# One tiled stretch a phase over eight PSUM banks, with an earlier softmax and a reordered start, in an attention-plus-MLP kernel

## The chip, the cores and the metric

One core of one Trainium2 chip. The metric is device microseconds of one execution, median of several; lower is better. The four runs of the kernel before agree within 0.3%. All spans, waits and instruction times come from the hardware profile.

## The reference, cut to what matters

```python
# x: (8, 8, 512, 64), state: (8, 8, 32, 64); per batch b and head h
a      = softmax(x @ state.T / 8)        # 512 x 32
xread  = a @ state                       # 512 x 64
a2     = softmax(state @ x.T / 8)        # 32 x 512
sread  = a2 @ x                          # 32 x 64
tokens = concat(xread, sread)            # 8 batches x 544 rows, 512 columns
out    = silu(tokens @ w_in) @ w_out     # w_in 512 x 2048, w_out 2048 x 512
```

The kernel never builds xread. As xread @ w_in = a @ (state @ w_in), it builds per batch a small product W1 = blockdiag(state) @ w_in (four quarters of 512 columns), transposes a, and uses W1 and aT in the first layer. "g" is silu of the first layer. The 32 sread rows of each batch are gathered and go through the MLP at the end, as a ninth small batch.

## The kernel before

Matmuls write to PSUM. The kernel has eight PSUM tiles of 128 x 512 fp32, called banks here: o0, o1, w0, w1, h0, h1, a0, a1. A bank can be written again only when an engine has copied its content out; that is what "frees a bank" means below. The instruction order on each engine is the order of these calls; nothing is rescheduled. ([...] marks cuts.)

```python
def w1_m(b, j, bks):        # one W1 quarter: 8 matmuls on 64x32 tiles of the array, two banks
    for kt in range(KT):
        for half in range(2):
            nc.tensor.matmul(bank[bks[half]][ds(32 * kt, 32), :], [...],
                             tile_position=(64 * half, 32 * kt))
def w1_e(b, j, bks, engs):  # copy both banks to W1 in SBUF, by ACT or DVE
    [...]
# sread_m: 32 matmuls on 128x32 tiles; sread_n: divide, on DVE; sread_t: transpose
# sc/scs: scores; ex/exs: exp on ACT; norm_s: row sums on DVE; norm_m: a = e / sum, DVE or POOL
# a_T: transpose of a on PE; a_Td: the same by DMA; x_Td: transpose of x by DMA

def g1(b, ft):              # a first-layer tile: 2 matmuls 128x512, then SiLU on ACT frees the h bank
    bk = bank[f"h{hctr[0] % 2}"]
    [...]
    nc.scalar.activation(g[b % 2][:, ft, :], bk[:], func=SILU, bias=0.0)

def o_e(b, tt, bk, eng="dve", [...]):   # copy a finished output bank to SBUF, then DMA it out
    [...]
    cp(eng, t[:, c0:c1], bank[bk][:, c0:c1])

def W1p(b, i):
    for j in range(2):
        w1_m(b, 2 * i + j, WP[j])           # WP = (("w0","w1"), ("h0","h1"))
    [...]

def phase(k, fill):          # 64 output matmuls of batch k; `fill` is put between them
    for tt in range(4):
        bk = ("o0", "o1")[tt % 2]
        for ft in range(16):
            g2(k, tt, ft, bk)
            for f in fill.get(16 * tt + ft, ()):
                f()
        o_e(k, tt, bk)

def att_tail(fill, b, s, a0, sg, dg):      # work for batch b, during phase b - 1
    add(fill, s, L(exs, b), L(W1p, b, 0))
    add(fill, s, L(norm_s, b, 0, 2), L(norm_m, b, "pool", 0, 2))
    add(fill, s, L(norm_s, b, 2, 2), L(norm_m, b, "dve", 2, 2))
    add(fill, s, L(nc.scalar.preload_act_table, SILU))
    add(fill, s + 14, L(W1p, b, 1), L(sread_m, b, "a1"), L(sread_n, b, "a1"))
    [...]
```

The prologue prepares batches 0 and 1 together (casts, transposes, scores, softmax). In the first phase (outputs of batch 0) W1 is built quarter by quarter for both batches.

The softmax here doesn't subtract the row's maximum and nothing guards it: scores larger than these inputs give would overflow.

## Time and profile before

| | before |
|---|---|
| time, median of 4 runs | 221.52 us |
| span in the profile | 219.67 us |
| first output matmul | 17.7 us |
| first phase / second phase | 28.0 / 26.95 us |
| a steady phase (third to sixth) | 23.14 us |

The page of the kernel before, busy time of the engines and the chain of waits that ended last:

```profile
PE 209.2 (95%) x1652; PEld 104.2 (47%) x1678; DVE 84.0 (38%) x171; ACT 131.5 (60%) x221; POOL 40.7 (19%) x78
...
PE 90%; DMA 2%; SPq 2%; issue 1%; ACT 1%; DVE 1%; POOL 0%
```

TensorE (PE) binds: it is hardly ever idle, and the chain runs through it. The busy share hides one thing: the profile models a 128x512 matmul as 379 ns, but starts are 0.216 us apart, so time on PE is counted by starts.

The timeline of PE around the two tiled stretches of one phase of the kernel before (start, duration, engine, line, operation, out<-in, shape, count, then idle time before it and what ended that):

```profile
95.75 0.59 PE L296 MATMUL ps_o<-w_out_sb,g 128*128 128x512 bf16 x2
96.28 0.41 PE L251 MATMUL ps_w<-w_in_sb,sbd 64*32 64x512 bf16 x8
96.50 0.56 PE L251 MATMUL ps_h<-w_in_sb,sbd 64*32 64x512 bf16 x8
97.23 2.97 PE L296 MATMUL ps_o<-w_out_sb,g 128*128 128x512 bf16 x13 [0.16 <-issue]
100.13 0.41 PE L251 MATMUL ps_w<-w_in_sb,sbd 64*32 64x512 bf16 x8
100.35 0.40 PE L251 MATMUL ps_h<-w_in_sb,sbd 64*32 64x512 bf16 x8
100.68 0.43 PE L218 MATMUL ps_a<-x_n,en 128*32 128x65 bf16 x32
```

The last full-array matmul before the first stretch starts at 95.97, the first tile at 96.28 instead of 96.19: entering costs 0.09 us, leaving about 0.10. Eight W1 tiles run together and cost 0.22. Counting by starts, the two stretches push their neighbours apart by 0.83 and 1.02 us. In the first of them 0.16 is neither: the second half of its h group starts at 96.66, when ACT's SiLU, which held that bank, has ended (96.61). (Each "x13" and the like misses one matmul record just after a stretch; its weight load is in the trace and was used.)

The timeline of PE at the start of the kernel before, three of its rows:

```profile
14.05 0.41 PE L251 MATMUL ps_o<-w_in_sb,sbd 64*32 64x512 bf16 x8
...
15.89 0.81 PE L272 MATMUL ps_h<-aT,W 128*128 128x512 bf16 x3
...
17.87 0.59 PE L296 MATMUL ps_o<-w_out_sb,g 128*128 128x512 bf16 x2
```

The busy times by stretch of the kernel before; the stretches begin at the first weight load of an output matmul of each phase (columns: stretch, its length, then busy time and instructions of PE, PE weight loads, DVE, ACT, POOL, granted clock, DMA share, GB/s):

```profile
0.00:17.66 17.66, 13.63 (x207) 11.06 (x208) 11.19 (x30) 11.26 (x22) 10.49 (x20) 1.00 0.89 201
17.66:45.66 28.00, 27.41 (x204) 11.55 (x207) 10.34 (x24) 16.27 (x30) 7.81 (x13) 1.00 0.96 168
45.66:72.61 26.95, 26.69 (x212) 12.55 (x215) 10.93 (x22) 19.87 (x31) 4.27 (x9) 1.00 0.59 167
72.61:95.75 23.14, 22.88 (x176) 10.47 (x178) 9.80 (x19) 15.27 (x24) 4.27 (x9) 1.00 0.45 126
```

### The profile page before, as it was taken

The page shows a single profiled execution, that of the slowest core. Times are in us where ns is not written, and L with a number is a line of the kernel's source. Part 1 is how long each engine was busy: PE and PEld are TensorE (multiplying, and loading weights), DVE is VectorE, ACT ScalarE, POOL GpSimd, SP SyncE. Part 2 cuts the span into 40 slices and gives each one's busy share as a digit, 9 for nine tenths or more (in the row PEclk, how much of TensorE's full clock was granted, in tenths as well). Part 3 has the DMA queues.
Part 4 walks back from the last instruction along what each step waited for, and adds up shares of the span by engine and source line. Part 5 has one row for each costly group of instructions (what it writes and reads, how often), then busy time and mean ns, then how long its engine had stood idle before and what let it go on. Part 6 is the DMA issues. An engine that isn't in the chain of part 4 may idle for free.

```text
span 219.7 us, 4129 instructions
## 1 busy us (share of the span) xinstructions
PE 209.2 (95%) x1652; PEld 104.2 (47%) x1678; DVE 84.0 (38%) x171; ACT 131.5 (60%) x221; POOL 40.7 (19%) x78
## 2 busy tenths in 40 slices
PE   7779999999999999999999999999999999999993
PEld 7555334453544444444444444444443444566552
DVE  4767321445730672139312841087107600111110
ACT  3873766669677846776477837692669277433210
POOL 1778222001600070007000610043001000000000
PEclk9999999999999999999999999999999999999999
DMA  6899999289551138512770269015411311111112
GB/s 204 229 179 169 206 232 188 42 225 286 191 120 51 48 97 189 196 48 51 187 243 3 69 169 276 16 51 145 95 48 51 97 48 51 49 48 48 51 48 96
DMA packets 36868, 26.56 MB, mean 121 GB/s; under 512 B 20848, under 2 KB 32368, under 8 KB 36848
## 3 DMA queue, kind: packets, MB, share of 16 engines
q1 hardware_dynamic: 30160, 20.39, 32.8%
q0 software_dynamic: 6128, 5.44, 14.8%
q10 hardware_dynamic: 560, 0.46, 0.6%
q8 instruction: 13, 0.21, 0.4%
q14 instruction: 7, 0.06, 0.1%
HBM read 17.30 MB, written 8.91 MB: 119 GB/s over the span
## 4 chain that ended last, share of the span: by engine, by line
PE 90%; DMA 2%; SPq 2%; issue 1%; ACT 1%; DVE 1%; POOL 0%
PE ps_o L296 49%; PE ps_h L272 25%; PE ps_w L296 4%; PE ps_h L283 3%; DMA x_f<-in_x_dram 2%; PE ps_w L251 2%; PE ps_h L251 2%; PE ps_a L218 1%; SPq L91 1%; PE ps_a L160 1%; PE ps_a L251 1%; ACT x_n L83 1%; PE ps_a L202 1%; DVE W L79 1%; POOL an L186 0%
## 5 line engine op out<-in xcount | busy, mean ns | idle before, releaser
L296 PE MATMUL ps_o<-w_out_sb,g 128*128 128x512 bf16 x462 | 124.8, 379 | 2.3 <-issue 1.7
L280 ACT ACTIVATE g<-ps_h 128x512 bf16<-128x512 f32 x128 | 75.7, 598 | 51.9 <-PE ps_h L272 49.6
L272 PE MATMUL ps_h<-aT,W 128*128 128x512 bf16 x248 | 73.6, 379 | 0.5 <-DVE W L79 0.3
L296 PEld LDWEIGHTS <-g 128*128 128x128 bf16 x512 | 47.9, 98 | 51.8 <-issue 1.6
L79 DVE COPY o_sb<-ps_o 128x512 f32<-128x512 f32 x30 | 20.6, 689 | 91.7 <-PE ps_o L296 76.7
L272 PEld LDWEIGHTS <-W 128*128 128x128 bf16 x256 | 24.3, 98 | 29.7 <-issue 1.6
L186 POOL TENSOR_TENSOR an<-en,rs 128x512 bf16<-128x512 bf16 x9 | 9.5, 1060 | 110.8 <-ACT W L83 56.6
L81 POOL CAST x_u<-x_f 128x256 bf16<-128x256 f32 x44 | 17.8, 447 | 4.5 <-DMA x_f<-in_x_dram 4.5
L79 DVE CAST W<-ps_w 128x512 bf16<-128x512 f32 x24 | 15.3, 679 | 3.5 <-PE ps_w L251 3.5
L83 ACT ACTIVATE W<-ps_h 128x512 bf16<-128x512 f32 x24 | 13.1, 603 | 0.1
L291 ACT ACTIVATE g_s<-ps_h 128x256 bf16<-128x256 f32 x16 | 6.1, 383 | 11.2 <-PE ps_h L283 11.2
L181 DVE TENSOR_REDUCE rs<-en 128x16 f32<-128x512 bf16 x16 | 10.5, 659 | 3.2 <-ACT en L171 3.1
L79 DVE CAST W<-ps_a 128x512 bf16<-128x512 f32 x7 | 4.8, 691 | 14.2 <-PE ps_a L251 14.2
L283 PE MATMUL ps_h<-xsT,w_in_sb 128*128 128x256 bf16 x64 | 9.6, 273 | 0.0
L296 PE MATMUL ps_w<-w_out_sb,g 128*128 128x512 bf16 x32 | 9.5, 379 | 0.1
L283 PEld LDWEIGHTS <-w_in_sb 128*128 128x128 bf16 x64 | 6.3, 98 | 4.1
L160 PEld LDWEIGHTS <-xT 128*128 128x128 bf16 x128 | 5.9, 98 | 4.3 <-DVE xT L79 0.4
L251 PEld LDWEIGHTS <-sbd 64*32 64x32 bf16 x256 | 3.1, 88 | 9.9 <-issue 9.4
L508 ACT ACT_TABLE_LOAD x6 | 7.7, 1283 | 0.1
L171 ACT ACT_TABLE_LOAD x6 | 7.7, 1283 | 0.1
L321 PEld LDWEIGHTS <-zeros 128*128 128x128 bf16 x86 | 6.6, 116 | 2.3 <-DVE zeros L335 1.2
L171 ACT ACTIVATE en<-ps_a 128x512 bf16<-128x512 f32 (+1 forms) x14 | 7.3, 564 | 0.4 <-PE ps_a L160 0.2
(66 smaller groups left out, 126.7 us busy)
## 6 DMA issues: line engine op xcount, KB each, us to landing
out_dram<-o_sb SPq DMA_DIRECT2D x32, 256.0 KB, 2.3
x_f<-in_x_dram SPq DMA_DIRECT2D x5, 1024.0 KB, 6.7
x_f<-in_x_dram SPq DMA_DIRECT2D x8, 256.0 KB, 4.5
w_in_sb<-in_moe_w_in_dram POOLq DMA_DIRECT2D x4, 512.0 KB, 9.6
w_out_sb<-in_moe_w_out_dram POOLq DMA_DIRECT2D x4, 512.0 KB, 11.9
x_f<-in_x_dram POOLq DMA_DIRECT2D x1, 1024.0 KB, 18.1
out_dram<-o_sb ACTq DMA_DIRECT2D x1, 256.0 KB, 2.5
st_nat<-in_state_dram POOLq DMA_DIRECT2D x6, 32.0 KB, 13.1
```

The lines of the kernel that those rows point to most:

```text
L79: nc.vector.tensor_copy(dst, src)
L81: nc.gpsimd.tensor_copy(dst, src)
L83: nc.scalar.activation(dst, src, func=COPY, bias=0.0)
L160: nc.tensor.matmul(v[:, kt % 2, :, c, :], xT[b % 2][:, kt, c, :], sbd[:, b, kt, :, :], start=True, stop=True, skip_group_check=True,)
L171: nc.scalar.activation(en[b % 2][:, :, :, ds(kt, n), :].rearrange("p h c k s -> p k (h c) s"), v[:, ds(kt % 2, n)], func=EXP, bias=0.0, sc ...
L181: nc.vector.tensor_reduce(v, en[b % 2][:, :, :, ds(kt, n), :], axis=AX, op=ADD)
L186: e.tensor_tensor(an[b % 2][:, :, :, ds(kt, n), :].rearrange("p h c k s -> p (h c) k s"), en[b % 2][:, :, :, ds(kt, n), :].rearrange("p h ...
L251: nc.tensor.matmul(bank[bks[half]][ds(32 * kt, 32), :], sbd[ds(64 * half, 64), b, kt, half, :], w_in_sb[ds(64 * half, 64), kt, ds(512 * j, ...
L272: nc.tensor.matmul(bk[:], W1[b % 2][:, half, ds(128 * ft, 128)], aT[b % 2][:, half, :, :], start=(half == 0), stop=(half == 1), skip_group ...
L280: nc.scalar.activation(g[b % 2][:, ft, :], bk[:], func=SILU, bias=0.0)
L283: nc.tensor.matmul(bk[:, 0:256], w_in_sb[:, kt, ds(128 * ft, 128)], xsT[:, kt, :, :, :], start=(kt == 0), stop=(kt == KT - 1), skip_group_ ...
L296: nc.tensor.matmul(bank[bk][:, c0:c1], src[:, ft, ds(128 * tt, 128)], w_out_sb[:, ft, c0:c1], start=(ft == 0), stop=(ft == 15), skip_group ...
```

## The change

Its intent: enter and leave the tiled shape once a phase instead of twice, by giving all four W1 quarters and sread a bank of their own (eight banks); have the softmax done well before the stretch; and start the first phase sooner, by taking batch 1 out of the prologue and loading the first weights ahead of batch 1's x. The diff cut to its core:

```diff
@@ later phases
-        def phase(k, fill):
-                bk = ("o0", "o1")[tt % 2]
+        TB = ("w0", "o0", "w1", "o1")        # four output banks in turn
+        def phase(k):
+                o_e(k, tt, TB[tt])
+                for f in fill.get((4 * k + tt,), ()):
+                    f()
+        def tiled(b, tt):                     # right behind the output copy tt
+            cur, nxt, third, srb = (TB[(tt + i) % 4] for i in range(4))
+            bks = ((srb, nxt), HB, AB, (third, cur))
+            for j in range(4):
+                w1_m(b, j, bks[j])
+            w1_e(b, 0, bks[0], ("act", "dve"))
+            sread_m(b, srb)
+            for j in range(1, 4):
+                w1_e(b, j, bks[j], ("act", "dve"))
+            sread_n(b, srb)
+        def soft(b):                          # all of it queued at once
+            exs(b)
+            nc.scalar.preload_act_table(SILU)
+            for q, e in enumerate(("pool", "dve")):
+                norm_s(b, 2 * q, 2)
+                norm_m(b, e, 2 * q, 2)
+            a_Td(b)
+            if b + 1 < B:
+                cast_xu(b + 1)
+        # step = 64 * phase + 16 * output + matmul. Per batch: x transpose, state transpose
+        # and x copy, scores, softmax, stretch (behind output number), sread transpose,
+        # first first-layer tile, steps between these tiles
+        plan = {
+            2: (None, None, 68, 74, 5, 108, 104, 1.5),
+            3: (98, 108, 119, 128, 9, 172, 166, 1.4),
+            4: (152, 172, 183, 188, 12, 225, 219, 1.5),
+        }
+        for b in range(5, B):
+            p = 64 * (b - 2)
+            plan[b] = (p + 20, p + 30, p + 46, p + 51, 4 * (b - 1), p + 97, p + 91, 1.5)
@@ start
-        nc.scalar.dma_start(st_f[0][:], ...)     # state of batch 1 came later, on SP
+        for b in range(2):
+            nc.scalar.dma_start(st_f[b][:], ...)
         ... x of batch 0 ...
-        ... x of batch 1 on SP ...
+        load_wi(0); load_wo(0); load_wi(1); load_wo(1)
+        load_x(1, nc.gpsimd, 0, 2)                # second half later, behind these
+        cp("act", st_nat[:, 1, :], st_f[1][:])    # ahead of everything else on ACT
@@ first phase: batch 1's casts, transposes, scores, softmax go here; W1 in pairs
+        w1_m(1, 1, AB)
+        w1_m(1, 2, HB)
+        w1_e(1, 2, HB, DA)
+        w1_e(1, 1, AB, DA)
   [...]
+        w1_m(0, 3, AB)
+        w1_m(1, 3, HB)
```

Also, batch 2's a is now transposed by DMA (a_Td) instead of on PE.

More of the change, by code (lines that the diff above doesn't have):

```diff
@@ L151, in x_Td, with x_nu @@
         )
+    def x_nu(b):
         nc.vector.tensor_copy(
@@ L326 @@
     with tc.manual_schedule():
-        nc.scalar.dma_start(st_f[0][:], state[0].rearrange("h ns d -> ns h d"))
+        for b in range(2):
+            nc.scalar.dma_start(st_f[b][:], state[b].rearrange("h ns d -> ns h d"))
         for kt in range(KT):
             load_x(0, nc.sync, kt, 1)
-        for kt in range(KT):
-            if kt == 2:
-                nc.sync.dma_start(st_f[1][:], state[1].rearrange("h ns d -> ns h d"))
-            load_x(1, nc.sync, kt, 1)
+        make_identity(nc, ident[:])
+        cp("pool", st_nat[:, 0, :], st_f[0][:])
+        load_wi(0)
+        load_wo(0)
+        load_wi(1)
+        load_wo(1)
+        load_x(1, nc.gpsimd, 0, 2)
         nc.vector.memset(zeros[:], 0.0)
@@ L338 @@
             nc.vector.memset(x_n[i][:, :, :, 1:131:129], 1.0)
-        make_identity(nc, ident[:])
         nc.scalar.preload_act_table(EXP)
@@ L346 @@
         HB = ("h0", "h1")
-        OB = XB
+        OB = ("w0", "w1", "o0", "o1")
         DA = ("dve", "act")
@@ L359, in exs, with xTs @@
         def exs(b):
-            for q in range(2):
-                ex(b, 2 * q, 2, AB[q])
+            ex(b, 0, 2, "a0")
+            ex(b, 2, 2, "a1")
+        def xTs(b, q, eng):
+            for kt in (2 * q, 2 * q + 1):
+                x_T(b, kt, AB[q])
+            x_Te(b, 2 * q, 2, AB[q], eng)
         def scs(b, q):
@@ L368 @@
         cast_x(0, "dve", (0,))
-        cp("pool", st_nat[:, 0, :], st_f[0][:])
+        cp("act", st_nat[:, 1, :], st_f[1][:])
         x_T(0, 0, XB[0])
@@ L373 @@
         st_T(0, "a1", "act", "dve")
-        cast_x(0, "dve", (2,), (0,))
-        cast_x(0, "pool", (2,), (1,))
-        cast_x(0, "dve", (3,), (0,))
-        cast_x(0, "pool", (3,), (1,))
-        cast_x(1, "pool", (0,), (1,))
-        load_wi(0)
-        load_wo(0)
+        cast_x(0, "dve", (2,))
         warm(8, "w1")
@@ L383 @@
         x_Te(0, 1, 1, XB[1], "act")
+        cast_x(0, "dve", (3,))
         sc(0, 0, SB[0])
         ex(0, 0, 1, SB[0])
-        warm(8, "w1")
+        warm(10, "w1")
         x_T(0, 2, XB[2])
         x_Te(0, 2, 1, XB[2], "act")
+        x_T(0, 3, XB[3])
+        x_Te(0, 3, 1, XB[3], "dve")
         sc(0, 1, SB[1])
         ex(0, 1, 1, SB[1])
-        warm(3, "w1")
-        x_T(0, 3, XB[3])
-        cast_x(1, "dve", (0,), (0,))
-        x_Te(0, 3, 1, XB[3], "dve")
-        warm(3, "o0")
+        warm(9, "o0")
         for kt in (2, 3):
@@ L398 @@
             ex(0, kt, 1, SB[kt])
-        cast_x(1, "dve", (1,))
-        cast_x(1, "act", (2,))
         norm_s(0, 0, 2)
         norm_m(0, "pool", 0, 2)
-        x_T(1, 0, "o0")
-        x_T(1, 1, "o0")
-        x_Te(1, 0, 2, "o0", "dve")
-        cp("act", st_nat[:, 1, :], st_f[1][:])
-        cast_x(1, "act", (3,))
-        warm(8, "a0")
-        st_T(1, "a1", "dve", "dve")
-        norm_s(0, 2, 2)
-        norm_m(0, "pool", 2, 2)
-        x_T(1, 2, "o1")
-        x_T(1, 3, "o1")
-        x_Te(1, 2, 2, "o1", "act")
-        warm(4, "a0")
-        sc(1, 0, "w0")
-        sc(1, 1, "w0")
-        ex(1, 0, 2, "w0")
-        warm(8, "a0")
-        sc(1, 2, "w1")
-        sc(1, 3, "w1")
-        ex(1, 2, 2, "w1")
-        nc.scalar.preload_act_table(SILU)
-        warm(8, "a0")
+        norm_s(0, 2, 2)
+        norm_m(0, "dve", 2, 2)
+        nc.scalar.preload_act_table(SILU)
+        st_T(1, "h0", "act", "act")
+        warm(6, "o0", 512)
+        w1_m(0, 0, ("w0", "w1"))
+        w1_m(1, 0, ("o0", "o1"))
+        w1_e(0, 0, ("w0", "w1"), ("act", "act"))
         a_T(0, (("a0", "dve"), ("a1", "dve")))
-        W1x(0, 0, ("o0", "o1"), DA)
-        load_wi(1)
-        load_wo(1)
+        w1_e(1, 0, ("o0", "o1"), DD)
+        warm(2, "h1", 512)
+        load_x(1, nc.gpsimd, 2, 2)
         load_wi(2)
         load_wo(2)
-        norm_s(1, 0, 2)
-        norm_m(1, "pool", 0, 2)
-        norm_s(1, 2, 2)
-        norm_m(1, "dve", 2, 2)
-        warm(6, "o0")
         g1(0, 0)
         g1(0, 1)
-        sread_m(0, "a0")
-        sread_n(0, "a0")
+        sread_m(0, "a1")
+        sread_n(0, "a1")
         g1(0, 2)
         g1(0, 3)
+        G2(0, 0)
+        sread_t(0, "a1", "dve")
+        G2(0, 1)
+        W1x(0, 1, AB, DA)
+        G2(0, 2)
+        G2(0, 3)
+        for i in range(4, 8):
+            g1(0, i)
+        cast_x(1, "dve", (0, 1))
+        cast_x(1, "dve", (2,))
+        cast_x(1, "pool", (3,))
         load_wi(3)
@@ L448 @@
             load_st(b)
-        G2(0, 0)
-        sread_t(0, "a0", "dve")
-        sread_m(1, "a1")
-        sread_n(1, "a1")
-        G2(0, 1)
-        sread_t(1, "a1", "dve")
-        a_T(1, (("a0", "dve"),))
-        G2(0, 2)
-        W1x(0, 1, AB, DA)
-        G2(0, 3)
-        W1x(1, 0, AB, DA)
-        for j in (1, 2, 3):
-            n = 3 * j - 3
-            g1(0, 4 * j)
-            g1(1, n)
-            W1x(1, j, AB, DA)
-            g1(0, 4 * j + 1)
-            g1(0, 4 * j + 2)
-            G2(0, 4 * j)
-            g1(0, 4 * j + 3)
-            G2(0, 4 * j + 1)
-            g1(1, n + 1)
-            if j == 3:
-                cast_xu(2, "dve", (0, 1))
-                cast_xu(2, "pool", (2, 3))
-                x_Td(2)
-                st_T(2, "a0", "dve", "dve")
-            G2(0, 4 * j + 2)
-            if j < 3:
-                W1x(0, j + 1, AB, DA)
-            g1(1, n + 2)
-            G2(0, 4 * j + 3)
+        G2(0, 4)
+        xTs(1, 0, "dve")
+        xTs(1, 1, "act")
+        G2(0, 5)
+        scs(1, 0)
+        scs(1, 1)
+        exs(1)
+        nc.scalar.preload_act_table(SILU)
+        W1x(0, 2, HB, DD)
+        G2(0, 6)
+        norm_s(1, 0, 2)
+        norm_m(1, "pool", 0, 2)
+        norm_s(1, 2, 2)
+        norm_m(1, "dve", 2, 2)
+        G2(0, 7)
+        g1(0, 8)
+        g1(0, 9)
+        w1_m(1, 1, AB)
+        w1_m(1, 2, HB)
+        w1_e(1, 2, HB, DA)
+        w1_e(1, 1, AB, DA)
+        G2(0, 8)
+        G2(0, 9)
+        a_T(1, (("a0", "act"),))
+        g1(0, 10)
+        g1(0, 11)
+        g1(1, 0)
+        G2(0, 10)
+        g1(1, 1)
+        w1_m(0, 3, AB)
+        w1_m(1, 3, HB)
+        w1_e(0, 3, AB, DA)
+        w1_e(1, 3, HB, DA)
+        G2(0, 11)
+        cast_xu(2, "dve", (0, 1))
+        cast_xu(2, "pool", (2, 3))
+        x_Td(2)
+        x_nu(2)
+        g1(0, 12)
+        g1(0, 13)
+        g1(1, 2)
+        G2(0, 12)
+        g1(0, 14)
+        G2(0, 13)
+        g1(0, 15)
+        g1(1, 3)
+        G2(0, 14)
+        st_T(2, "a0", "dve", "dve")
+        g1(1, 4)
+        G2(0, 15)
+        g1(1, 5)
         for tt in range(4):
@@ L483 @@
         load_x(3, nc.sync)
-        g1(1, 9)
-        WP = (("w0", "w1"), ("h0", "h1"))
-        def W1p(b, i):
-            for j in range(2):
-                w1_m(b, 2 * i + j, WP[j])
-            for j in range(2):
-                w1_e(b, 2 * i + j, WP[j], DD if j == 0 else ("act", "act"))
-        def phase(k, fill):
-            for tt in range(4):
-                bk = ("o0", "o1")[tt % 2]
-                for ft in range(16):
-                    g2(k, tt, ft, bk)
-                    for f in fill.get(16 * tt + ft, ()):
-                        f()
-                o_e(k, tt, bk)
@@ L504, in add @@
-        def add(fill, step, *fs):
-            fill.setdefault(int(step), []).extend(fs)
+        TB = ("w0", "o0", "w1", "o1")
+        fill = {}
+        def add(step, *fs):
+            fill.setdefault(step if isinstance(step, tuple) else int(step), []).extend(fs)
         def L(f, *a):
             return lambda: f(*a)
-        def att_head(fill, b, s0, s1):
-            add(fill, s0, L(st_T, b, "a0", "dve", "dve"))
-            add(fill, s0, L(x_Td, b))
-            if 4 < b + 1 < B:
-                add(fill, s0, L(load_x, b + 1, nc.sync))
-            add(fill, s1, L(scs, b, 0))
-            add(fill, s1 + 2, L(scs, b, 1))
@@ L518, in att_tail @@
-        def att_tail(fill, b, s, a0, sg, dg):
-            add(fill, s, L(exs, b), L(W1p, b, 0))
-            add(fill, s, L(norm_s, b, 0, 2), L(norm_m, b, "pool", 0, 2))
-            add(fill, s, L(norm_s, b, 2, 2), L(norm_m, b, "dve", 2, 2))
-            add(fill, s, L(nc.scalar.preload_act_table, SILU))
-            add(fill, s + 14, L(W1p, b, 1), L(sread_m, b, "a1"), L(sread_n, b, "a1"))
-            if b == 2:
-                add(fill, a0, L(a_T, b, (("a0", "act"),)))
-            else:
-                add(fill, s, L(a_Td, b))
-            add(fill, a0 + 2, L(sread_t, b, "a1", "dve"))
-            for i in range(16):
-                add(fill, sg + dg * i, L(g1, b, i))
@@ L532 @@
-        fill = {}
-        for i in range(10, 16):
-            add(fill, i - 10, L(g1, 1, i))
-        add(fill, 2, L(scs, 2, 0))
-        add(fill, 3, L(scs, 2, 1))
-        att_tail(fill, 2, 6, 30, 35, 1.8)
-        add(fill, 6, L(cast_xu, 3), L(load_x, 4, nc.sync))
-        att_head(fill, 3, 37, 58)
-        phase(1, fill)
-        for k in range(2, 7):
-            fill = {}
-            att_tail(fill, k + 1, 0, 24, 35, 1.8)
-            if k + 2 < B:
-                add(fill, 0, L(cast_xu, k + 2))
-                att_head(fill, k + 2, 34, 56)
-            phase(k, fill)
@@ L551 @@
-        fill = {}
+        def phase(k):
+            for tt in range(4):
+                for ft in range(16):
+                    g2(k, tt, ft, TB[tt])
+                    for f in fill.get(64 * k + 16 * tt + ft, ()):
+                        f()
+                o_e(k, tt, TB[tt])
+                for f in fill.get((4 * k + tt,), ()):
+                    f()
+        def tiled(b, tt):
[8 more added lines that the diff above has]
+            sread_n(b, srb)
@@ new lines, in sread_x @@
+        def sread_x(b, tt):
+            sread_t(b, TB[(tt + 3) % 4], "dve")
+        def soft(b):
+            exs(b)
+            nc.scalar.preload_act_table(SILU)
+            for q, e in enumerate(("pool", "dve")):
[5 more added lines that the diff above has]
+        plan = {
[3 rows of a table added]
+        }
+        for b in range(5, B):
+            p = 64 * (b - 2)
+            plan[b] = (p + 20, p + 30, p + 46, p + 51, 4 * (b - 1), p + 97, p + 91, 1.5)
@@ new lines @@
+        for b, (sx, ss, sq, se, tl, sr_, sg, dg) in plan.items():
+            if sx is not None:
+                add(sx, L(x_Td, b))
+                add(ss, L(x_nu, b), L(st_T, b, "a0", "dve", "dve"))
+            if 3 < b + 1 < B:
+                add(sx or se, L(load_x, b + 1, nc.sync))
+            add(sq, L(scs, b, 0))
+            add(sq + 2, L(scs, b, 1))
+            add(se, L(soft, b))
+            add((tl,), L(tiled, b, tl))
+            add(sr_, L(sread_x, b, tl))
+            for i in range(16):
+                add(sg + dg * i, L(g1, b, i))
@@ L552 @@
+        for i in range(6, 16):
+            add(64 + i - 6, L(g1, 1, i))
+        add(65, L(sread_m, 1, "a1"), L(sread_n, 1, "a1"))
+        add(67, L(sread_t, 1, "a1", "dve"))
         for i in range(16):
-            add(fill, 2 + 3 * i, L(g1, 8, i))
-        phase(7, fill)
+            add(448 + 2 + 3 * i, L(g1, 8, i))
+        for k in range(1, 8):
+            phase(k)
         for ft in range(16):
```

## The prediction

> **What bounds it now.** TensorE: the page has PE 95% busy, and 90% of the chain of waits. In the timeline 128x512 matmuls follow each other every 0.216 us, whatever their modelled 379 ns. By windows:
> - Prologue, to the first g matmul at 15.9 us. Chain: x landing until 9.3, batch 1's casts and transposes, the second softmax multiply on POOL (ends 13.5), a transposes, aT copies 0.76, a W1 copy 0.69.
> - First phase 15.9–45.9, dense; 10 first-layer tiles of batch 1 are done in it. Second phase to 73.0.
> - Five steady phases of 23.15: 96 x 0.216 = 20.73, scores 0.46, transposes 0.12, and two tiled stretches, which push apart the matmuls around them by 0.83 (16 W1 tiles) and 1.02 us (16 W1, 32 sread). A further W1 group of 8 costs 0.227; the rest is entering and leaving. The Trainium skill ("TensorEngine Tiling (Array Packing)", Key Properties) says that changing tiling mode drains the engine; the trace agrees.
>
> **What the change does.**
> 1. One stretch a phase. Ideally 1.45 us against 1.85. But sread's bank must first be copied out by ACT (0.60; about 0.1 late), and the next output bank waits behind two DVE copies (0.69 each, at the edge). I take 1.57: 0.27 a phase, 1.6 in six.
> 2. Batch 2's a transpose moves from PE to DMA: 0.45.
> 3. Batch 1 leaves the prologue; weights are issued at 4.2 instead of 8.1. Estimate from the trace's durations: last x chunk 6.7, batch 0's a normalized 11.2, first g matmul 12.5, first output matmul 14.7 instead of 17.9: 3.3 us sooner.
> 4. That work returns in the first phase: 16 transposes 0.9, scores 0.46; pairing W1 there saves 0.4. Four first-layer tiles (0.43 each) and one sread move to the second phase.
> 5. New PE waits in the first phase, added up along the order: four first-layer tiles in a row limited by SiLU, 0.2; EXP load, two exps, SILU load (1.28+1.1+1.28) ahead of the SiLUs that free both h banks for batch 1's paired W1, 1.3; the 1.0 us aT copy on ACT ahead of two SiLUs before batch 1's first tile, 0.9; h banks before the second pair 0.3; others 0.2. About 3. Batch 1's x lands behind four weight loads (2.5–4.1 us each before): estimate 21 us, needed at 21.5; 0.3 on average.
>
> At equal progress the first phase ends where it did, or up to 2 us sooner if the order hides more than I see. Sum: 0.5 (first phase) + 0.45 + 1.6 + some credit for hidden waits: about 3 us.
>
> **Prediction: 218.4 us (215.8 to 220.6).** Faster by over 2%: 0.28; within 2%: 0.69; slower: 0.03.
>
> **What would show it.** Timeline: first g matmul near 12.5; steady phases near 22.85; one stretch a phase, costing 1.57. Waits: PE waits for ACT or DVE some 3 us in the first phase, worst before batch 1's paired W1 and its first tile. DMA: batch 1's second half of x lands near 21 us, the last w_out quarter near 31.
>
> **What would make it wrong.** POOL-issued weight loads crawling while batch 0's x moves, so that the first W1 waits, or batch 1's x landing after 22 us: slower by 1–2. ACT done earlier than in my sum, so that step 5's waits vanish: 216. The four W1 groups waiting for banks, so that the merged stretch costs what two did: 220. PE gaps lowering the granted clock (1.00 everywhere now).

## The result, and the profile after

| | before | after |
|---|---|---|
| time, median of 4 runs | 221.52 us | 226.51 us |
| ratio (95% interval) | | 1.0225 (1.020 to 1.0249) |
| first output matmul | 17.66 us | 15.75 us |
| first phase / second phase | 28.0 / 26.95 | 30.35 / 30.19 |
| third, fourth, fifth, sixth phase | 23.14, 23.15, 23.15, 23.14 | 23.03, 24.69, 22.95, 22.95 |
| first-layer tiles done before the second phase | 26 | 22 |

A ratio is the mean time of one kernel's fast runs over that of the other's of the same rounds, so it is not quite the ratio of the medians. All four runs were fast ones, granted clock 0.99 to 1.00. The changed kernel is 2.25% slower: the prediction had the wrong sign.

The page after, the same two lines:

```profile
PE 211.3 (94%) x1649; PEld 105.2 (47%) x1649; DVE 83.9 (37%) x175; ACT 132.8 (59%) x220; POOL 40.6 (18%) x78
...
PE 75%; DMA 9%; POOL 5%; ACT 4%; DVE 3%; issue 2%; ACTq 0%; POOLq 0%; DVEq 0%
```

The busy shares look as before, but only 75% of the chain is PE now; DMA, POOL, ACT and DVE hold 21% of it. The busy times by stretch of the kernel after, beginning at the same events:

```profile
0.00:15.75 15.75, 12.58 (x163) 9.46 (x163) 9.48 (x25) 8.75 (x18) 8.31 (x16) 1.00 0.95 178
15.75:46.10 30.35, 27.88 (x192) 12.29 (x190) 12.37 (x29) 18.92 (x30) 9.89 (x16) 1.00 0.93 180
46.10:76.29 30.19, 28.37 (x249) 13.45 (x248) 11.53 (x25) 21.03 (x34) 4.26 (x9) 1.00 0.61 157
76.29:99.32 23.03, 23.03 (x179) 10.61 (x178) 9.52 (x19) 15.86 (x26) 4.27 (x9) 1.00 0.48 127
99.32:124.01 24.69, 22.90 (x180) 10.83 (x179) 9.54 (x20) 17.41 (x28) 4.26 (x9) 1.00 0.49 118
```

Two things stand out. The first two phases are 5.6 us longer together, against 1.9 us won at the start. And the fourth phase has the same PE busy time as its neighbours but is 1.74 us longer than the fifth: pure waiting.

The timeline of PE around the stretch of batch 2, in the second phase:

```profile
59.92 0.41 PE L253 MATMUL ps_w<-w_in_sb,sbd 64*32 64x512 bf16 x8 [1.23 <-DVE o_sb L79]
60.13 0.41 PE L253 MATMUL ps_h<-w_in_sb,sbd 64*32 64x512 bf16 x8
60.35 0.41 PE L253 MATMUL ps_a<-w_in_sb,sbd 64*32 64x512 bf16 x8
60.57 0.41 PE L253 MATMUL ps_o<-w_in_sb,sbd 64*32 64x512 bf16 x8
61.09 0.43 PE L220 MATMUL ps_w<-x_n,en 128*32 128x65 bf16 x32
61.45 2.12 PE L298 MATMUL ps_w<-w_out_sb,g 128*128 128x512 bf16 x9
64.04 0.39 PE L274 MATMUL ps_h<-aT,W 128*128 128x512 bf16 x1 [0.48 <-DMA aT<-an]
```

The stretch itself is as planned: four W1 groups 0.22 apart, sread, out. But its first matmul waits 1.23 us for DVE to copy an output out of bank w0, although that output was finished about 4 us earlier. The timeline of DVE shows why:

```profile
56.52 0.69 DVE L183 TENSOR_REDUCE rs<-en 128x16 f32<-128x512 bf16 x1 [6.44 <-ACT en L173]
...
57.41 0.63 DVE L183 TENSOR_REDUCE rs<-en 128x16 f32<-128x512 bf16 x1
...
58.36 0.91 DVE L188 TENSOR_TENSOR an<-en,rs 128x512 bf16<-128x512 bf16 x1
59.19 0.68 DVE L79 COPY o_sb<-ps_w 128x512 f32<-128x512 f32 x1
```

DVE had been idle for 6.44 us, held at the head of its queue by the softmax's first sum, which needed ACT's exp. The output copy was queued behind the five softmax instructions (two reciprocals are left out above), so it ran at 59.19 when its data had been ready since about 55. ACT, for its part, was late because the exps stood behind the SiLUs and a table load (the timeline of ACT after):

```profile
53.98 0.60 ACT L282 ACTIVATE g<-ps_h 128x512 bf16<-128x512 f32 x1
54.59 1.28 ACT L173 ACT_TABLE_LOAD   x1
55.89 1.08 ACT L173 ACTIVATE en<-ps_a 128x512 bf16<-128x512 f32 x2
56.99 1.28 ACT L534 ACT_TABLE_LOAD   x1
```

Batch 4's stretch in the fourth phase shows the same. DVE, then PE:

```profile
101.47 0.69 DVE L183 TENSOR_REDUCE rs<-en 128x16 f32<-128x512 bf16 x1 [8.93 <-ACT en L173]
...
104.11 0.68 DVE L79 COPY o_sb<-ps_o 128x512 f32<-128x512 f32 x1
```

```profile
104.84 0.41 PE L253 MATMUL ps_o<-w_in_sb,sbd 64*32 64x512 bf16 x8 [1.68 <-DVE o_sb L79]
```

The six stretches of the kernel after cost, by starts, 2.92, 1.64, 3.37, 1.65, 1.64 and 1.64 us (batches 2 to 7), against 1.85 for a pair of stretches before. Four are 0.2 us better than before; batches 2 and 4 lose 1.07 and 1.52.

The timeline of PE at the start of the kernel after:

```profile
12.03 0.41 PE L253 MATMUL ps_w<-w_in_sb,sbd 64*32 64x512 bf16 x8 [0.78 <-DMA w_in_sb<-in_moe_w_in_dram]
...
13.65 1.14 PE L274 MATMUL ps_h<-aT,W 128*128 128x512 bf16 x4
...
15.96 0.59 PE L298 MATMUL ps_w<-w_out_sb,g 128*128 128x512 bf16 x2
```

The first w_in quarter is issued at 4.33 instead of 8.09 us, but lands at 11.98 instead of 13.63, so of the 3.3 us that the prediction hoped for 1.9 came. At equal progress (four first-layer tiles of 2 x 0.216 us and one sread of 0.5 us are still owed) the end of the first phase is 2.7 us later than before: 46.10 + 1.73 + 0.52 - 45.66. That is one profile. Five experiments below (oe_on_act, stretch_later, fit_later, fit2_later, b3_earlier) keep this start and first phase unchanged; in the six profiles together the phase ends between 45.95 and 46.95, so the loss is 2.5 to 3.5 us.

### The profile page after: what moved, and what is told of

It is laid out like the page before. It is cut to its first block, busy times and chain, and to the rows that moved or that the text cites. A ratio compares the mean times of both kernels' runs of the same rounds, so it can differ in the third digit from the quotient of the medians.

```text
span 224.5 us, 4127 instructions
## 1 busy us (share of the span) xinstructions
PE 211.3 (94%) x1649; PEld 105.2 (47%) x1649; DVE 83.9 (37%) x175; ACT 132.8 (59%) x220; POOL 40.6 (18%) x78
## 4 chain that ended last, share of the span: by engine, by line
PE 75%; DMA 9%; POOL 5%; ACT 4%; DVE 3%; issue 2%; ACTq 0%; POOLq 0%; DVEq 0%
PE ps_o L298 23%; PE ps_h L274 22%; PE ps_w L298 21%; DMA x_f<-in_x_dram 5%; PE ps_h L285 3%; DMA aT<-an 2%; DMA st_f<-in_state_dram 2%; POOL st_nat L105 2%; POOL an L188 1%; PE ps_a L162 1%; DVE rs L183 1%; ACT L173 1%; PE ps_o L253 1%; ACT g L282 1%; ACT en L173 1%
## 5 line engine op out<-in xcount | busy, mean ns | idle before, releaser
L274 PE MATMUL ps_h<-aT,W 128*128 128x512 bf16 x256 | 75.0, 379 | 1.7 <-ACT g L282 1.2
L298 PE MATMUL ps_w<-w_out_sb,g 128*128 128x512 bf16 x256 | 72.1, 379 | 0.0
L298 PE MATMUL ps_o<-w_out_sb,g 128*128 128x512 bf16 x256 | 67.5, 379 | 0.0
L79 DVE COPY o_sb<-ps_w 128x512 f32<-128x512 f32 (+1 forms) x17 | 11.4, 673 | 46.0 <-PE ps_w L298 45.8
L79 DVE COPY o_sb<-ps_o 128x512 f32<-128x512 f32 x16 | 10.9, 686 | 23.9 <-PE ps_o L298 23.8
L253 PEld LDWEIGHTS <-sbd 64*32 64x32 bf16 x256 | 4.2, 90 | 12.5 <-issue 11.0
L83 ACT ACTIVATE W<-ps_o 128x512 bf16<-128x512 f32 x6 | 3.6, 604 | 9.7 <-PE ps_o L253 9.7
L79 DVE COPY sbd<-ps_a 64x128 bf16<-64x128 bf16 x13 | 3.7, 287 | 12.9 <-PE ps_a L119 11.2
L79 DVE CAST W<-ps_a 128x512 bf16<-128x512 f32 x9 | 6.2, 684 | 6.0 <-PE ps_a L253 6.0
L83 ACT ACTIVATE W<-ps_w 128x512 bf16<-128x512 f32 x8 | 4.8, 607 | 5.4 <-PE ps_w L253 5.3
```

The costliest lines, as they stand in the source:

```text
L79: nc.vector.tensor_copy(dst, src)
L83: nc.scalar.activation(dst, src, func=COPY, bias=0.0)
L253: nc.tensor.matmul(bank[bks[half]][ds(32 * kt, 32), :], sbd[ds(64 * half, 64), b, kt, half, :], w_in_sb[ds(64 * half, 64), kt, ds(512 * j, ...
L274: nc.tensor.matmul(bk[:], W1[b % 2][:, half, ds(128 * ft, 128)], aT[b % 2][:, half, :, :], start=(half == 0), stop=(half == 1), skip_group ...
L298: nc.tensor.matmul(bank[bk][:, c0:c1], src[:, ft, ds(128 * tt, 128)], w_out_sb[:, ft, c0:c1], start=(ft == 0), stop=(ft == 15), skip_group ...
```

## The experiments

Each call of runs had its own chip, so what is compared with the kernel before is its ratio of the same call; where a text below compares with the changed kernel, that is its 226.51 us of the first chip, and the phase lengths and stretches of the profiles carry the argument. Labels in the expectations: oe_on_act, stretch_later, old_start, prologue_st, fit_later, fit2_later, old_start_fit, old_start_fit2, b3_earlier, start_and_fit, start_and_fit2 and unpaired are these experiments in turn.

Theory Q (queue order): the output copies that free the stretch's banks are queued on DVE behind the sooner softmax of batches 2 and 4, so PE waits. Theory P: the new start loses at equal progress, because batch 1's work and new waits stand in the first phase. The rival, theory M: a stretch that wants all eight banks at once is too demanding by itself, wherever the softmax is.

### Four output copies moved from DVE to ACT

```diff
-                o_e(k, tt, TB[tt])
+                o_e(k, tt, TB[tt], "act" if (k, tt) in ((1, 0), (1, 1), (2, 3), (3, 0)) else "dve")
```

> The changed kernel with four of its output copies (outputs 0 and 1 of the second phase, 3 of the third, 0 of the fourth) on ACT instead of DVE; nothing else moved. Theory Q (queue order: these copies stand on DVE behind the sooner softmax of batches 2 and 4, which waits for EXP load and exps, so the stretch's banks come free late): the stretches of batches 2 and 4, which cost 2.92 and 3.37 us against 1.64 of the others, fall to about 2.0 and 2.1, and the kernel to about 224.3 us. Theory M (a stretch over all eight banks is itself too demanding there): those two stay near 3 us and the kernel at 226.5.

Measured: 225.02 us (223.97 to 226.23), ratio 1.0164. The stretches of batches 2 and 4 fell to 1.94 and 2.44 us, the other four stayed at 1.64. In the waits of PE the copies are now ACT's, and shorter, but the a transpose is waited for twice, and longer than before (columns: engine, tile and line, released by: us in total, times, longest):

```profile
PE ps_h L274 <- DMA aT<-an: 1.6, 2, 1.0
...
PE ps_o L253 <- ACT o_sb L83: 0.7, 1, 0.7
...
PE ps_w L253 <- ACT o_sb L83: 0.2, 1, 0.2
```

So 1.9 us of the stretches' waits went, as Q says, which speaks against M; but much of the gain turned into the next wait, since aT comes no sooner. The second and the fourth phase together are only 0.6 us shorter (29.40 and 24.90 us), and the profiled run, the slowest of the four, has the span of the changed kernel. By the medians 1.5 us reached the total, less than expected.

### The two stretches one output later (a bad edit)

```diff
-            2: (None, None, 68, 74, 5, 108, 104, 1.5),
+            2: (None, None, 68, 74, 6, 124, 120, 1.2),
-            4: (152, 172, 183, 188, 12, 225, 219, 1.5),
+            4: (152, 172, 183, 188, 13, 241, 235, 1.2),
```

> The changed kernel with the stretches of batches 2 and 4, their sread transposes and first-layer tiles 16 steps (one output) later, the softmax where it is. Theory Q: both stretches cost 1.64 like the others, the 0.6 us wait for the a transpose of batch 2 goes too: about 222.9 us (to 223.5 if first-layer tiles crowd the phase's end). Theory M: 226.5, the waits move along.

Measured: 235.84 us, ratio 1.069 (one of its four runs was slow and is left out of the ratio; the median of the three fast ones is 235.36). Both theories were wrong about this run, because the edit did more than it meant: batch 2's first-layer tiles now ran into batch 3's softmax, and on ACT a table load, two exps and another table load stood between their SiLUs. PE waited 7.8 us for SiLUs that free h banks, 3.3 at once. The total tells nothing of Q or M, but shows what it costs here when a block of first-layer tiles has not ended before the next batch's softmax begins. The two moved stretches cost 2.59 and 3.06 us, for a reason that fit_later shows below.

### The old start with the new later phases

```diff
 (the kernel before, with the changed kernel's TB, tiled, soft, plan and phase)
-        for i in range(6, 16):
-            add(64 + i - 6, L(g1, 1, i))
-        add(65, L(sread_m, 1, "a1"), L(sread_n, 1, "a1"))
-        add(67, L(sread_t, 1, "a1", "dve"))
+        for i in range(10, 16):
+            add(64 + i - 10, L(g1, 1, i))
```

> Prologue and first phase of the kernel before (10 first-layer tiles of batch 1 and both sreads done in it), all later phases of the changed kernel. Theory P (the new start is a loss of about 2.7 us at equal progress): first phase ends near 45.7 us; and with 6 instead of 10 SiLUs ahead of batch 2's softmax its stretch costs at most 1.9 and the wait for its a transpose goes: about 222.1 us. If the new start is neutral and only the later phases cost, 224.8 or more.

Measured: 221.61 us, ratio 1.0007: level with the kernel before. The second phase began at 45.99 us. Batch 2's stretch cost 1.78 instead of 2.92, the wait for its aT went, and batch 4's stayed at 3.38. Undoing the start and first phase thus takes off 4.9 us (4.6 between the profiles): 2.4 in the progress by the end of the first phase (48.35 at equal progress against 45.99), 1.14 in batch 2's stretch and 0.64 in the wait for aT; the last 0.4 is not traced. That the second and third come from the four SiLUs less before batch 2's exps is what was expected, but no run varies these alone.

### The state of batch 1 behind batch 0's x

```diff
-        for b in range(2):
-            nc.scalar.dma_start(st_f[b][:], ...)
+        nc.scalar.dma_start(st_f[0][:], ...)
         for kt in range(KT):
             load_x(0, nc.sync, kt, 1)
+        nc.sync.dma_start(st_f[1][:], ...)
 (and the ACT cast of st_f[1] moved from ahead of the first x copy to behind the exps)
```

> The changed kernel with the load of batch 1's state behind batch 0's x, and its cast on ACT after the exps instead of first. Theory W (the first W1 waits for the first w_in quarter, which lands at 12.0 us): the softmax of batch 0 is done 1.2 us sooner but the first g matmul moves from 13.4 by less than 0.4: 226.1 to 226.5 us. Theory S (the state's late landing held ACT and through it the start): first g matmul near 12.3, 225.2 us.

Measured: 224.70 us (224.38 to 225.28), 1.8 less than the changed kernel. First g matmul at 12.57 (weight load), near theory S. ACT copied the first x transpose at 5.03 instead of 6.32 us, where it had idled 2.59 us for the state to land. Of the gain 0.8 us came in the first phase (29.56 against 30.35), which the edit leaves as it was. But in this profile w_in's first quarter also landed at 10.0 us. In the nine other profiles of kernels with the new start, with and without this edit, it landed between 11.7 and 13.1, and three of those had the same edit (11.85, 11.94 and 12.56). So the edit's gain is real in the medians, but how much of the first matmul's gain came from ACT and how much from that landing stays open.

### The stretches one output later, fitted

```diff
-            2: (None, None, 68, 74, 5, 108, 104, 1.5),
-            3: (98, 108, 119, 128, 9, 172, 166, 1.4),
-            4: (152, 172, 183, 188, 12, 225, 219, 1.5),
+            2: (None, None, 68, 74, 6, 124, 114, 0.9),
+            3: (98, 102, 119, 128, 9, 172, 166, 1.4),
+            4: (152, 172, 183, 188, 13, 236, 226, 1.1),
 (and batch 5's state transpose and x copy at p + 22 instead of p + 30)
```

> The changed kernel with the stretches of batches 2 and 4 one output later, and this time their first-layer tiles so close (one per 0.9 and 1.1 steps, at once after the stretch) that all are done before the next batch's softmax, and the next batch's state transpose ahead of the stretch. Theory Q (output copies queued on DVE behind the softmax): both stretches cost 1.64, the wait for the a transpose goes, no new wait of ACT: about 222.9 us. Theory M (eight banks): still near 226.

Measured: 226.21 us: no gain, the stretches cost 2.59 and 3.05. Taken alone this looked like theory M. The timelines say otherwise. PE first, then DVE:

```profile
62.80 0.40 PE L253 MATMUL ps_h<-w_in_sb,sbd 64*32 64x512 bf16 x8
63.66 0.41 PE L253 MATMUL ps_a<-w_in_sb,sbd 64*32 64x512 bf16 x8 [0.46 <-DVE sbd L79]
```

```profile
62.41 0.69 DVE L154 COPY x_n<-x_u 128x2048 bf16<-128x2048 bf16 x1 [1.50 <-POOL x_u L81]
63.02 0.58 DVE L79 COPY sbd<-ps_a 64x128 bf16<-64x128 bf16 x2
```

The state transpose of batch 3 now sat in bank a0, its copy-out was queued on DVE behind the x copy, and that one waited for POOL's casts. It is the same fault in a second place, made by moving the stretch behind this x copy (stretch_later had it too): a bank's release queued behind something that waits for another engine.

### The same, with the x copy behind the stretch

```diff
-                add(ss, L(x_nu, b), L(st_T, b, "a0", "dve", "dve"))
+                add({3: 102, 5: 214}.get(b, ss), L(st_T, b, "a0", "dve", "dve"))
+                add({3: 113, 5: 226}.get(b, ss), L(x_nu, b))
```

> fit_later without its new wait: there the two later stretches cost 2.59 and 3.05 us because DVE stood at the copy of batch 3's (5's) x, which waits for POOL's casts, with the copies that free bank a0 behind it. Here that x copy is queued behind the stretch. Theory Q2 (what counts is which DVE work stands ahead of a bank's release): both stretches cost 1.64 to 1.7; third and fourth phases at 23.0, second near 28.9; 223.0 us or, with the slow start of fit_later's profile, 223.9. Theory M (stretches over eight banks late in a phase are dear): stays near 226.

Measured: 224.07 us (222.36 to 224.28), ratio 1.0095. All six stretches cost 1.64 to 1.65. The second phase fell to 28.90 us, the fourth to 23.12, as expected: 2.86 us less in these two than in the changed kernel. The total fell by 2.4, to just above the upper figure named; the first phase of this profile was 0.7 us longer than the changed kernel's.

### Old start, last dear stretch later

Without the mend of the x copy:

> Start of the kernel before with the later phases of the changed one, and batch 4's stretch one output later, its first-layer tiles done before batch 5's softmax. Theory Q: the last dear stretch (3.38) costs 1.64: 219.9 us, 0.6% below the kernel before. Theory M: as old_start, 221.6.

Measured: 221.59 us median, but one of its four executions took 558.8 us and was the one profiled: its matmuls started 0.621 us apart instead of 0.216, with SiLUs of the usual 597 ns. It is set aside as slow; the clock on its record is 1.00, so the cause is not known. The three fast runs have a median of 221.41 and give a ratio of 0.9985, so most of its predicted gain did not come. No profile of a fast run was taken; by its order it carries the same queueing of the x copy that cost batch 4's stretch its gain in fit_later.

With the mend (batch 5's x copy behind the stretch), five rounds:

> old_start with batch 4's stretch one output later and the x copy of batch 5 behind it. Theory Q2: no dear stretch is left; 221.6 less 1.7 is 219.9 us, ratio 0.992 to the kernel before. Theory M: 221.3 like old_start_fit.

Measured: 220.01 us (219.52 to 220.34), ratio 0.9925 (0.9912 to 0.9939). This version is 0.75% faster than the kernel before: clear of the noise. The timeline of PE around batch 4's stretch in it:

```profile
102.39 0.41 PE L253 MATMUL ps_w<-w_in_sb,sbd 64*32 64x512 bf16 x8
102.62 0.40 PE L253 MATMUL ps_h<-w_in_sb,sbd 64*32 64x512 bf16 x8
102.83 0.40 PE L253 MATMUL ps_a<-w_in_sb,sbd 64*32 64x512 bf16 x8
103.05 0.60 PE L253 MATMUL ps_o<-w_in_sb,sbd 64*32 64x512 bf16 x8
103.58 0.43 PE L220 MATMUL ps_w<-x_n,en 128*32 128x65 bf16 x32
```

Eight banks at once, and no wait but the 0.2 us of every free stretch: 1.64 us. Theory M falls; the steady phases of this version take 22.95 to 23.12 us, against 23.14 of the kernel before.

### A free stretch moved nearer to its softmax

The opposite dose: make the fault where there was none.

```diff
-            3: (98, 108, 119, 128, 9, 172, 166, 1.4),
+            3: (98, 108, 119, 128, 8, 172, 166, 1.4),
```

> The changed kernel with the one stretch of batch 3 moved 16 steps nearer to its softmax (15 steps behind it instead of 31), nothing else. Theory Q: this stretch, free of waits until now (1.64), costs 3.4 to 3.9, because the output copy that must free its bank now stands behind the softmax on DVE: 228.4 us. Theory M: stays 1.64 and 226.5.

Measured: 228.10 us, ratio 1.029, and the stretch cost 3.23 instead of 1.64. The timeline of PE:

```profile
81.50 0.38 PE L253 MATMUL ps_w<-w_in_sb,sbd 64*32 64x512 bf16 x1
83.28 0.41 PE L253 MATMUL ps_w<-w_in_sb,sbd 64*32 64x512 bf16 x7 [1.41 <-DVE o_sb L79]
```

Here only the fourth group waits, for the copy of the output just finished (bank w0), and on DVE that copy ran at 82.54 behind batch 3's softmax. The sign and nearly the size are as Q said.

### The mended start and stretches together

fit_later with the prologue_st edit and `a_T(1, (("a0", "dve"),))` instead of "act" (that is, batch 1's transposed a is copied out by DVE):

> fit_later, with batch 1's state loaded behind batch 0's x (as prologue_st, which took 1.8 us off) and batch 1's a transpose copied out by DVE instead of ACT in the first phase (its wait for ACT there was 0.9 us): about 220.3 us if these gains add up; 222 or more if the first phase's waits only move to the next ACT copy.

Measured: 224.48 us, ratio 1.0127. The stretches had fit_later's fault. The a transpose on DVE gained nothing in the first phase (29.50 us against 29.56 of prologue_st): the wait of 0.9 us before batch 1's first tile fell to 0.42, but the transpose itself now waited 0.41 for POOL's half of the softmax. With the x copy mended:

> start_and_fit with the same mend: 224.5 less 2.4 is 222.1 us. If the new start, even mended, were no loss, it would come under old_start_fit2 (219.9); theory P says that it stays about 2 us above it, because batch 1's transposes, scores and SiLU waits stand in the first phase.

Measured: 222.50 us (221.48 to 223.43), ratio 1.004. It stays 2.5 us above old_start_fit2, which has the same later phases but for batch 2's entry: the new start is a loss even with these mends.

### The pairs of W1 in the first phase undone

```diff
-        w1_m(1, 1, AB)
-        w1_m(1, 2, HB)
-        w1_e(1, 2, HB, DA)
-        w1_e(1, 1, AB, DA)
+        W1x(1, 1, AB, DA)
 (W1x(1, 2, AB, DA) behind g1(0, 11); W1x(0, 3, AB, DA) in place of the second pair;
  W1x(1, 3, AB, DA) behind g1(1, 2); base: start_and_fit2)
```

> start_and_fit2 with the two pairs of W1 quarters of the first phase (batch 1's second and third; batch 0's and 1's fourth) undone: four single stretches, all in the a banks, none waits for an h bank. Theory H (the second half of a pair waits for h banks that SiLUs still hold: 0.69 + 0.27 + 0.31 us in start_and_fit's trace): these go, two more stretches cost 0.42, so the first phase is about 0.8 us shorter (28.7 to 29.5 us, by how late the weights land) and the kernel at 221.7. If pairing pays as meant, the kernel gets 0.4 slower: 222.9.

Measured: 221.89 us (221.42 to 222.51), 0.6 under its base, but the two ranges overlap (and it was run on another chip), so the time is inconclusive. Its first phase took 28.94 us, in the expected range, against 30.25 of its base; but by starts 0.94 of this difference came ahead of the first pair, where nothing was edited (waits of 0.54 for w_in and 0.43 for a cast of x that this profile did not have). So at most about 0.4 is the edit's. The waits for h banks before W1 are gone from PE's list, and these are in it:

```profile
PE ps_a L204 <- POOL an L188: 0.8, 1, 0.8
PE ps_w L298 <- ACT g L282: 0.5, 1, 0.5
```

By starts the pairs' three waits made 1.27 us. Now the output matmuls wait 0.59 for a SiLU, and the a transposes 0.75 longer for POOL's half of the softmax. So most of that wait is not the pair's: ACT and POOL are not done by then, after an EXP load, two exps and a SILU load of batch 1's softmax, which the change had put into the first phase.

## Why the prediction was wrong

Point by point, in us, counted at equal progress; minus is a gain:

| term | predicted | shown |
|---|---|---|
| six stretches | -1.6 | -0.2 in each of four, +1.07 (batch 2), +1.52 (batch 4): +1.8 |
| batch 2's a transpose by DMA | -0.45 | -0.45, and +0.64 waiting for aT |
| start of the first phase | -3.3 | -1.9 |
| first phase, work moved in and waits (steps 4 and 5) | +4.2 | +4.6 |
| credit for hidden waits | about -1.9 | none |
| sum | about -3 | +4.7 (spans: +4.8) |

**What bounds it**: right, and the 0.216 us cadence held.

**The stretch itself**: the mechanism was right and the size close. It costs 1.64 where I took 1.57 and the ideal was 1.45. The wait inside the stretch is 0.19 where I had 0.12, and it stands elsewhere: not before sread, but in the fourth W1 group, whose second bank is that of the output just finished and still has to be copied out by DVE (in batch 3's stretch 84.16 to 84.36).

**The step that failed** is step 1's "0.27 a phase, 1.6 in six". I costed one steady phase, whose output copies are at the head of DVE's queue, and multiplied by six. The plan of batches 2 and 4 is not like the others: from softmax to stretch there are 22 and 20 matmul steps, against 29 to 32 for batches 3 and 5 to 7. I had listed DVE's copies as the next limit ("two DVE copies, at the edge"), but looked only at their durations, not at what stands ahead of them in the queue. The Trainium skill ("TensorE: Matmul & The Clock Gate", Architectural detail: the array is 16× 32×32, not 1× 128×128, on queue depths) says that "ACT/DVE are strict FIFO", and this trace agrees: 6.44 us idle at a sum that waited for ACT, the last 1.3 of them with a copy behind it whose data had been ready since about 55.2. What was in the diff, and what I did not do, was to walk DVE's order from each softmax to each stretch. The chain is ACT SiLU backlog, 1.28 us EXP load, 1.08 of exps, 2.7 us of DVE softmax, 0.68 of copy. Taking the copies out of DVE's queue eased it (oe_on_act), it was made where it was not (b3_earlier), and removed (fit2_later, old_start_fit2).

**"At equal progress the first phase ends where it did, or up to 2 us sooner"** failed too: it ends 2.7 us later. First, this line does not follow from the prediction's own terms. Steps 4 and 5 add up to 4.2 us (0.9 + 0.46 - 0.4 of work; 0.2 + 1.3 + 0.9 + 0.3 + 0.2 + 0.3 of waits), against 3.3 won at the start: 0.9 later, and not the 0.5 sooner that went into the sum. With the rest of the credit, 1.9 us of "the order hides more than I see" were booked as a gain, and nothing was hidden. Without them the same terms give a gain of about 1 us. Second, the first w_in quarter needs 7.5 to 9 us from issue to landing in its new place, in all traces but one; in the old place, where the x loads had almost ended, it was 5.5 us. That cost 1.4 of the 3.3. "What would make it wrong" had named this, and batch 1's x after 22 us (its second half landed at 23.2, not 21), but at 1 to 2 us.

The waits that step 5 names were all found at their places in the trace: 0.42 (four tiles in a row; predicted 0.2), 0.69 + 0.27 (first pair; 1.3), 0.90 (before batch 1's first tile; 0.9), 0.31 (second pair; 0.3). With those that it did not name, such as 0.42 at a second run of four tiles and 0.44 for the cast of batch 1's x, PE waits 4.1 us in this phase by starts, against 0.4 before.

**Batch 2's a transpose** off PE saved its PE time (0.45: eight transposes from 57.63 to 58.08 in the kernel before) but added a wait for the DMA of 0.64. In old_start, with six SiLUs of batch 1 before the exps instead of ten, the wait is gone.

**The granted clock** did not matter: 1.00 in every stage of both profiles.

Open: what spreads the landing of the first w_in quarter from 10.0 to 13.1 us with much the same issues ahead of it; and the first phase's remaining loss in start_and_fit2, which I ascribe to moved work (16 transposes, scores) and to the waits for ACT and POOL behind batch 1's softmax, but took apart only in part.

## What to carry to other kernels

When a wait is moved to an in-order engine's queue, cost it by what stands behind it: a softmax queued early on DVE holds every later copy, and a copy that frees a PSUM bank is worth more than its duration. Check this at every place where a plan's distances differ, not only at the steady one; here it broke at the irregular first entries. Before taking work out of a prologue, ask whether the phase that gets it has slack on every engine the work needs; here ACT with its table loads had as little as PE. And add up your own terms: hidden waits that no term shows are no gain.

## What the Trainium skill lacked or had wrong

- "TensorEngine Tiling (Array Packing)", Key Properties, says that changing mode drains the engine but gives no cost. Here entering the 64x32 shape from full-array matmuls costs 0.09 us and leaving it about 0.10 us, by starts; the W1-to-sread change (64x32 to 128x32) about 0.09 to 0.1. One stretch instead of two saved 0.2 us a phase (0.16 of wait for an h bank went too, and 0.19 for an output bank came).
- "TensorE: Matmul & The Clock Gate", Back-to-back issue gap, gives about 131 ns per matmul as the sustained rate at 512 columns with weight loads. Here it is 216 ns throughout, at granted clock 1.00, with a weight load for each matmul. That section has this figure for an isolated gap only; the page is not of one mind, as its "Step-by-step: what each phase is for" gives 215.7 as measured back to back.
- "ScalarE: Activation LUTs", What ACT_TABLE_LOAD costs, gives 2.66 us per switch, of which 1.38 are a drain. Here the load took 1.28 us, as there, but began 0.01 us after the SiLU before it ended, and the exp began 0.02 us after the load: no drain shows.
- "DMA: Bandwidth & Descriptors", Anatomy of one DMA, SWDGE (gpsimd) path, has a fit of 2.0 us plus bytes over 436e3 per us: 1 MB of fp32 read gives an estimate of 4.4 us (its table of measured loads has 6.15 us for 1 MB). The first w_in quarter (1 MB of fp32, cast to 0.5 MB) took 5.5 us in the kernel before, and 7.5 to 9 in nine of ten profiles of the new start (5.9 in the tenth), with batch 0's x and the next weight loads in flight. The page has no figure for a load that shares the engines so.
- The queue note in "TensorE: Matmul & The Clock Gate" does not say what a strict first-in, first-out queue costs TensorE when a copy that frees a PSUM bank stands behind an instruction that waits. Here it was 1.07 and 1.52 us a stretch.
